# The second MLP of a pooled-attention and two-MLP kernel as seven block products, on tiles of 256 tokens

## The chip, the cores and the metric

The kernel runs on one core of a Trainium2 chip. The metric is the device time of one execution in microseconds; three runs of the kernel before gave 1746.33, 1746.94 and 1750.57 us, median 1746.94. The engines are TensorE (PE; its weight loads are shown apart as PEld), VectorE (DVE), ScalarE (ACT), GpSimd (POOL) and SyncE (SP, which only issues DMAs here).

## The reference

```python
def _attn_ref(q, k, v):                 # (8, 8, 576, 64): batch, heads, sequence, head
    k_p = k.reshape(B, H, Sp, 8, D).mean(axis=3)     # 72 pooled keys and values
    v_p = v.reshape(B, H, Sp, 8, D).mean(axis=3)
    scores = (1 / np.sqrt(D)) * np.matmul(q, k_p.transpose(0, 1, 3, 2))
    ...softmax...
    return np.matmul(attn, v_p)

def _moe_ref(x, w_in, w_out):           # x (4608, 512), w_in (512, 2048), w_out (2048, 512)
    h = x @ w_in
    g = np.where(h >= 1, h, np.where(h <= -1, 0, (h + 1) ** 2 / 4))
    return g @ w_out

def _moe2_ref(x, w_in, w_out):          # same shapes
    h = x @ w_in
    g = h * (1 / (1 + np.exp(-h)))
    return g @ w_out
```

The attention's output, 4608 tokens of 512 numbers, goes through the first MLP and then through the second. The moe weights come as 64-bit floats, which the kernel reads as pairs of 32-bit words.

## The kernel before

**Numbers.** Every big matrix is held as two f16 tiles, a high part and a low part, scaled by powers of two. A product of two such matrices is three matmuls into the same PSUM tile: high by high, high by low, low by high (`three`, lines 115 to 118). So all matmul counts below have a factor 3.

**Tiles and stages.** Tokens go in nine tiles of 512 (N). The attention prepares x for a tile of the first MLP. For each of 16 chunks m of 128 hidden numbers, `emit_h` makes 12 matmuls of 512 columns into a PSUM tile "h" (two buffers), ScalarE and VectorE make the activation g from it and split g into f16 halves, and three chunks later (LAG) `emit_yA` or `emit_yB` adds 12 more matmuls of 512 columns to the four output accumulators y0 to y3. So a tile is 384 matmuls. The main loop (line 1014) goes over the 16 x 18 steps of both MLPs without a break: the first nine tiles are the first MLP (`pre_A`, `min_A`, `mid_A`, `post_A`, `split_g`), the next nine the second (`act_B`, `split_g`). The first MLP's output goes to DRAM (`evac_yA`, ydram) and comes back a tile at a time (`tile_B`: one load "yin", four maxima, the scale by way of a pair of matmuls "all" on TensorE in `all_max`, and four splits). `big`, where y goes out and yin comes in, has one buffer.

**Weights of the second MLP.** They are prepared in steps during the first MLP (list `todo`, line 1009, spread over six tiles by the count in line 1047): load a piece of 1 MB (512 x 256 of w_in, 256 x 512 of w_out), five passes on ScalarE and VectorE that turn the 64-bit words into f32 (s0 to s4), then s5: scale and round on ScalarE, subtract on GpSimd, and write both halves to DRAM (d3, d4). For w_in each of eight pieces has its own scale, taken from a maximum that step s1 accumulates; for w_out one scale holds for all, and each piece is read twice, once to look at its maximum (`look`) and once to be converted. When the attention is done, its memory becomes free, and 8.4 MB of prepared weights are loaded into SBUF (lines 1041 to 1046).

**What sets the order.** The program is written in the order above; a scheduler of the framework then sets each engine's order, which an engine keeps: an instruction that waits holds up all that stand behind it. SP issues the DMAs in its own order.

Of the kernel before, what the change touches and what calls it, by code (L numbers as in the profile page):

```python
# [9 lines left out]
F32 = mybir.dt.float32  # L10
F16 = mybir.dt.float16
# [22 lines left out]
def tile_pooled_attention_two_mlps(  # L34
# [40 lines left out]
    w1p = ctx.enter_context(tc.tile_pool(name="w1", bufs=1))  # L75
# [76 lines left out]
    def w_scale(e, s, g):  # L152


        ts(g.bitcast(I32), g.bitcast(I32), 0x7FF00000, op0=ALU.bitwise_and)
        bits(s, g, -8.0, 2060)
        bits(e, g, 8.0, -1784)

    def steps(piece, dst, scale, loaded, mx=None, seen=None):
# [40 lines left out]
        def s5():  # L200
            x, s = t["x"], scale()
            hi, lo, *end = dst()
            nc.scalar.activation(out=x, in_=x, func=AF.Copy, scale=s)
# [72 lines left out]
    def weight_whole(w, e, dst, pieces):  # L276
# [16 lines left out]
        def scale():  # L293
# [30 lines left out]
    def split_steps(src, m4, e, s):  # L324
        hi, lo = new_x()

        def scale():
            m1 = sm.tile([128, 1], F32, tag="m1", name="m1")
            nc.vector.tensor_reduce(out=m1, in_=m4, axis=AX.X, op=ALU.max)
            to_scale(e, s, m1, FLOOR)  # L330

        return (hi, lo), [scale] + [lambda c=c: split(hi[:, c], lo[:, c], src[:, c], s) for c in range(KD)]
# [268 lines left out]
    w2 = [w1p.tile([128, 2, KF, 128], F16, name=f"wb{d}") for d in range(KD)]  # L601
# [7 lines left out]
    e1, e2, e3, e4 = col(len(cuts1)), col(KD), col(PIECES), col()  # L609
    e1m, e3m = col(), col()  # L610
# [36 lines left out]
    d3 = [dram.tile([128, KD, DFF], F16, name=f"d3{i}") for i in range(2)]  # L647
    d4 = [dram.tile([128, KF, DM], F16, name=f"d4{i}") for i in range(2)]

    def staged(views):  # L650
        shape = list(views[0].shape)
        t = [gp.tile([128, 2, N], F16, tag="g", name="hl").rearrange("p a n -> p (a n)") for _ in views]
        t = [x.rearrange("p (a b) -> p a b", a=shape[1]) for x in t]

        def end():
            for x, v_ in zip(t, views):
                nc.sync.dma_start(out=v_, in_=x)
        return t[0], t[1], end

    def dst3(p):  # L660
        hi, lo, end = staged([d[:, :, p * CW:(p + 1) * CW] for d in d3])
        if p < PIECES - 1:
            return hi, lo, end

        def both():
            end()
            largest(e3m, e3)
        return hi, lo, both

    def dst4(i):  # L670
        return staged([d[:, 2 * i:2 * i + 2] for d in d4])
# [23 lines left out]

    def load_y(t):
        y = big.tile([128, KD, N], F32, tag="big", name="yin")
        nc.sync.dma_start(out=y, in_=ydram[t])
        return y

    def tile_B(t):

        r = XT[NTILE + t] = small(e=1, s=1, c1=PIECES, ge=1, sg=1)
        held = {}

        def load():
            held["y"] = load_y(t)
            held["m4"] = sm.tile([128, KD], F32, tag="m4", name="m4b")

        def look(c):  # L710
            abs_max(held["m4"][:, c:c + 1], held["y"][:, c], AX.X)

        def more():
            r["x"], held["st"] = split_steps(held["y"], held["m4"], r["e"], r["s"])
            held["st"].pop(0)()
            ts(r["c1"], e3, r["e"], 2.0 ** -28, ALU.mult, ALU.mult)
            ts(r["ge"], e3m, r["e"], 2.0 ** -4, ALU.mult, ALU.mult)
            bits(r["sg"], r["ge"], -1.0, 254)

        return ([load] + [lambda c=c: look(c) for c in range(KD)] + [more]  # L720
                + [lambda: held["st"].pop(0)()] * KD)
# [82 lines left out]
    def act_B(s, r):  # L804
        ps = h_t.pop(s)
        p = s % KF // (KF // PIECES)
        g = g32_t[s] = up.tile([128, N], F32, tag="g", name="g32")
        nc.scalar.activation(out=g, in_=ps, func=AF.Silu, scale=r["c1"][:, p:p + 1])  # L808

    def split_g(s, r):  # L810
# [3 lines left out]
        if s < NTILE * KF:  # L814
            nc.scalar.copy(out=gh, in_=g)  # L815
            return nc.vector.tensor_tensor(out=gl, in0=g, in1=gh, op=ALU.subtract)  # L816
        else:
            nc.scalar.activation(out=gh, in_=g, func=AF.Copy, scale=r["sg"])  # L818
# [33 lines left out]
    def emit_yB(s, w):  # L852

        t, m = divmod(s, KF)
        if m == 0:
            new_acc(t)
# [243 lines left out]
```

## Time and profile before

| | us |
|---|---|
| median of three runs (1746.33 to 1750.57) | 1746.94 |
| the profiled execution, own time | 1752.34 |
| its span | 1750.4 |
| TensorE busy | 1620.5 (93%) |
| VectorE busy | 904.8 (52%) |
| ScalarE busy | 776.8 (44%) |
| GpSimd busy | 220.7 (13%) |

The first matmul of the second MLP starts at 990.1 us. Busy times are sums over instructions and average over quite different stages: attention and weight preparation run beside the first MLP until some 870 us, and GpSimd is idle after that. Matmuls are pipelined, so their durations (0.38 us for 512 columns) overlap; the time per matmul is the distance of their starts.

### The profile page before, as it was taken

Reading aid. Unit: us, or ns where it says so; the run is one execution under the profiler, and the core shown is the slowest. Engines: PE = TensorE matmul, PEld = TensorE weight load, DVE = VectorE, ACT = ScalarE, POOL = GpSimd, SP = SyncE. Lnnn points to the kernel's source line nnn. Section 1 sums busy time; section 2 is a strip of 40 time slices with the busy share of each in tenths; the row PEclk is TensorE's granted clock in tenths of the full one; section 3 lists DMA queues with packets and bytes.
Section 4 is the critical chain, followed back from the end, with each engine's and each line's share of the span. In section 5 each row is a group of like instructions: output and inputs, shape, how many; then the busy total and the mean of one; then the engine's idle time right before and its main releaser. Section 6 shows DMA issues by size and latency. Waiting matters only on the chain.

```text
span 1750.4 us, 21833 instructions
## 1 busy us (share of the span) xinstructions
PE 1620.5 (93%) x8594; PEld 757.5 (43%) x8594; DVE 904.8 (52%) x1714; ACT 776.8 (44%) x1215; POOL 220.7 (13%) x195
## 2 busy tenths in 40 slices
PE   4763789999998999999999999999999999999998
PEld 3321334444444444444444444444444444444443
DVE  8797778878788597886535331212121312122111
ACT  3575455665646556475434433333332323233232
POOL 5733412121221112112100000000000000000000
PEclk8786789999999999999999999999999999999999
DMA  9414655655659346342241010000000000000000
GB/s 283 127 57 119 138 130 128 149 127 125 154 125 269 89 131 148 90 120 61 55 187 49 10 63 25 25 25 24 25 25 25 25 24 25 25 25 25 0 25 24
DMA packets 206086, 144.55 MB, mean 83 GB/s; under 512 B 153120, under 2 KB 170528, under 8 KB 204832
## 3 DMA queue, kind: packets, MB, share of 16 engines
q1 hardware_dynamic: 205984, 143.16, 30.8%
q8 instruction: 67, 1.10, 0.3%
q14 instruction: 35, 0.29, 0.0%
HBM read 88.08 MB, written 27.26 MB: 66 GB/s over the span
## 4 chain that ended last, share of the span: by engine, by line
PE 64%; DVE 18%; ACT 7%; DMA 6%; issue 2%; POOL 1%; SPq 0%; ACTq 0%; POOLq 0%; DVEq 0%
PE hps L116 10%; PE hps L118 10%; PE hps L117 10%; PE y L863 7%; PE y L862 7%; PE y L861 7%; DVE sum L388 5%; PE y L116 3%; PE y L118 3%; PE y L117 3%; DVE g L816 2%; DVE g L762 2%; DMA raw<-in_moe_w_in_dram 1%; DVE xf L189 1%; DVE xf L195 1%
## 5 line engine op out<-in xcount | busy, mean ns | idle before, releaser
L819 DVE SCALAR_TENSOR_TENSOR g<-g,tsg,g 128x512 f16<-128x512 f32 x144 | 108.2, 751 | 479.6 <-ACT g L818 478.5
L808 ACT ACTIVATE g<-hps,tc 128x512 f32<-128x512 f32 x144 | 99.0, 687 | 504.7 <-PE hps L118 502.1
L116 PE MATMUL hps<-xh,wa 128*128 128x512 f16 x576 | 226.3, 393 | 40.0 <-DVE g L762 22.7
L117 PE MATMUL hps<-xl,wa 128*128 128x512 f16 x576 | 226.2, 393 | 0.0
L118 PE MATMUL hps<-xh,wa 128*128 128x512 f16 x576 | 224.3, 391 | 1.8 <-POOL wa L205 1.8
L116 PE MATMUL hps<-xh,wch 128*128 128x512 f16 x576 | 218.3, 379 | 0.0
L117 PE MATMUL hps<-xl,wch 128*128 128x512 f16 x576 | 218.3, 379 | 0.0
L118 PE MATMUL hps<-xh,wcl 128*128 128x512 f16 x576 | 218.3, 379 | 0.0
L861 PE MATMUL y<-wdh,g 128*128 128x512 f16 x576 | 218.3, 379 | 0.0
L862 PE MATMUL y<-wdl,g 128*128 128x512 f16 x576 | 218.3, 379 | 0.0
L863 PE MATMUL y<-wdh,g 128*128 128x512 f16 x576 | 218.3, 379 | 0.0
L117 PE MATMUL y<-g,wb 128*128 128x512 f16 x544 | 206.9, 380 | 2.3 <-DVE g L816 1.7
L118 PE MATMUL y<-g,wb 128*128 128x512 f16 x544 | 206.8, 380 | 0.0
L116 PE MATMUL y<-g,wb 128*128 128x512 f16 x544 | 203.5, 382 | 0.4 <-ACT y L849 0.4
L753 ACT ACTIVATE u<-u,trsg 128x512 f32<-128x512 f32 x128 | 91.9, 719 | 87.7 <-DVE u L89 87.7
L762 DVE SCALAR_TENSOR_TENSOR g<-hps,tc,u 128x512 f32<-128x512 f32 x136 | 101.5, 746 | 54.8 <-ACT u L753 53.8
L816 DVE TENSOR_TENSOR g<-g,g 128x512 f16<-128x512 f32 x128 | 97.2, 760 | 50.6 <-ACT g L815 49.1
L747 ACT ACTIVATE u<-hps,tch 128x512 f32<-128x512 f32 x128 | 87.0, 680 | 72.6 <-PE hps L118 72.3
L815 ACT CAST g<-g 128x512 f16<-128x512 f32 x128 | 78.5, 614 | 83.4 <-DVE g L762 81.0
L89 DVE TENSOR_SCALAR u<-u 128x512 f32<-128x512 f32 x144 | 75.8, 526 | 66.5 <-ACT u L747 66.1
L818 ACT ACTIVATE g<-g,tsg 128x512 f16<-128x512 f32 x144 | 103.8, 721 | 4.5
L117 PEld LDWEIGHTS <-wa 128*128 128x128 f16 x576 | 57.9, 101 | 96.1 <-issue 37.3
(171 smaller groups left out, 2047.2 us busy)
## 6 DMA issues: line engine op xcount, KB each, us to landing
raw<-in_moe_w_out_dram SPq DMA_DIRECT2D x24, 1024.0 KB
raw<-in_moe_w_in_dram SPq DMA_DIRECT2D x10, 1024.0 KB
raw<-in_k_dram SPq DMA_DIRECT2D x32, 288.0 KB
raw<-in_v_dram SPq DMA_DIRECT2D x32, 288.0 KB
y<-y SPq DMA_DIRECT2D x36, 256.0 KB
yin<-y SPq DMA_DIRECT2D x9, 1024.0 KB
out_dram<-osb SPq DMA_DIRECT2D x36, 256.0 KB
qt<-in_q_dram SPq DMA_DIRECT2D x32, 256.0 KB
```

Source lines behind the costliest of these rows:

```text
L116: nc.tensor.matmul(out=acc, lhsT=wh, rhs=xh, start=start, stop=False)
L117: nc.tensor.matmul(out=acc, lhsT=wh, rhs=xl, start=False, stop=False)
L118: nc.tensor.matmul(out=acc, lhsT=wl, rhs=xh, start=False, stop=stop)
L753: nc.scalar.activation(out=u_t[s], in_=u_t[s], func=AF.Square, scale=0.5 if s < KF else r["rsg"])
L762: return nc.vector.scalar_tensor_tensor(out=g, in0=h_t.pop(s), scalar=c_A(r, "c1", s), in1=u_t.pop(s), op0=ALU.mult, op1=ALU.max)
L808: nc.scalar.activation(out=g, in_=ps, func=AF.Silu, scale=r["c1"][:, p:p + 1])
L816: return nc.vector.tensor_tensor(out=gl, in0=g, in1=gh, op=ALU.subtract)
L818: nc.scalar.activation(out=gh, in_=g, func=AF.Copy, scale=r["sg"])
L819: nc.vector.scalar_tensor_tensor(out=gl, in0=g, scalar=r["sg"], in1=gh, op0=ALU.mult, op1=ALU.subtract)
L861: nc.tensor.matmul(out=a, lhsT=h_, rhs=w[0][:, m], start=st, stop=False)
L862: nc.tensor.matmul(out=a, lhsT=h_, rhs=w[1][:, m], start=False, stop=False)
L863: nc.tensor.matmul(out=a, lhsT=l_, rhs=w[0][:, m], start=False, stop=sp)
```

## The change

For a tile of 256 tokens the second MLP's two products are taken in blocks. x (512 x 256) and a piece of w_in (512 x 256) are cut into 2 x 2 blocks; sums and differences of the blocks are formed (`comb_a` for the weights, `comb_b` for x), seven block products are made instead of eight (`product`), and VectorE adds them up to the four blocks of h (c11, c12, c21, c22). The same is done for the output: sums of the blocks of g (z1 to z4, on GpSimd), seven products into y0 to y3 (`py`), and `evac_yB` adds them up.

The weights' combinations are made once, in the first MLP's time, and kept in DRAM: seven blocks of 256 columns a piece where there were four, as two halves. w_in now has one scale for all, with a look at each piece as w_out had. The first half of w_out's pieces (wd0 to wd3) and all of w_in's (wc0 to wc7) are loaded when the attention's memory is free, the other half (wd4 to wd7) when the first MLP's weights are released. The second MLP is a loop of its own: 18 tiles of 256 tokens, in two groups of four pieces each; the output products of a group are placed between the h products of the next.

```diff
-    w1p = ctx.enter_context(tc.tile_pool(name="w1", bufs=1))
+    wctx = ExitStack()
+    w2p = wctx.enter_context(tc.tile_pool(name="w2", bufs=1, side="right"))
+    w1p = wctx.enter_context(tc.tile_pool(name="w1", bufs=1, side="right"))
...
+            if fill:
+                fill(x)
+                return
...
+    def comb_a(z, a11, a12, a21, a22):
+        plus(z[1], a21, a22)
+        minus(z[2], z[1], a11)
+        minus(z[3], a11, a21)
+        minus(z[0], a12, z[2])
...
+    def staged(d, i, parts):
+        to = [[gp.tile([128, 2, N], F16, tag="g", name="hl").rearrange("p a n -> p (a n)") for _ in range(2)]
+              for _ in range(2)]
+        for a, b, x in parts:
...
+            nc.scalar.copy(out=hi, in_=x)
+            minus(lo, x, hi)
+        for j in range(2):
+            for k_, n in ((0, 4), (1, 3)):
+                nc.sync.dma_start(
...
+    def fill3(i, x):
+        b = x.rearrange("p (h c) (m f) -> p m h c f", h=2, m=2)
...
+        comb_a(z, b[:, 0, 0], b[:, 0, 1], b[:, 1, 0], b[:, 1, 1])
+        staged(d3, i, [(0, 2, b[:, 0]), (2, 3, z[0]), (3, 4, b[:, 1, 1]),
+                       (4, 7, z4[:, 1:4].rearrange("p n c f -> p (n c f)"))])
...
-    loads3, work3 = weight_in(moe2_w_in, e3, dst3, cuts3)
+    loads3, looks3, work3 = weight_whole(moe2_w_in, e3, fill3, [((0, KD), c) for c in cuts3])
...
+        def look():
+            m = sm.tile([128, 1], F32, tag="m1", name="m1")
+            abs_max(m, held["y"])
+            to_scale(r["e"], r["s"], m, FLOOR, 12)
...
+        return [load, look, sums_, lambda: part(0, 2, lambda: held["b"][:, :, 0]),
+                lambda: part(2, 3, lambda: held["b"][:, 1, 1]), lambda: part(3, 7, lambda: held["z"])]
...
+        def product(n, i):
+            p, tag = ((ps_h, "h"), (ps_a, "a"))[n // 2 % 2]
+            ps = p.tile([128, 4, 128], F32, tag=tag, name="hb")
+            for j in range(4):
+                w = w3[4 * q + j]
+                for k_ in range(2):
+                    three(ps[:, j], w[:, 0, i, k_], w[:, 1, i, k_], xh[:, i, k_], xl[:, i, k_],
+                          j == 0 and k_ == 0, j == 3 and k_ == 1)
+            return ps
...
+        def halves_of(i, x):
+            to = gt[i] = pool.tile([128, 2, N], F16, tag="g", name="g16")
+            split(to[:, 0], to[:, 1], x.rearrange("p j n -> p (j n)"), r["sg"])
...
+        nc.scalar.copy(out=u, in_=product(0, 0))
+        add(c11, u, product(1, 1))
+        act(c11)
+        halves_of(0, c11)
+        y(1)
+        add(u, u, product(2, 5))
+        y(1)
+        add(v, u, product(3, 6))
+        y(1)
+        p5 = product(4, 4)
+        add(c22, v, p5)
+        act(c22)
+        add(u, u, p5)
+        halves_of(3, c22)
...
+        plus(z1, c12, c22)
+        minus(z3, c11, c12)
+        minus(z2, z1, c11)
...
+            for j in range(4):
+                f, w = slice(128 * j, 128 * j + 128), w4[4 * q + j]
+                three_r(out, gh[:, f], gl[:, f], w[:, 0, i], w[:, 1, i], first and j == 0, last and j == 3)
...
+    todo = loads3 + looks3 + flat(work3) + loads4 + looks4 + flat(work4)
...
     wctx.close()
+    b2 = bctx.enter_context(tc.tile_pool(name="b2", bufs=1, side="right", reuse_waits="tile"))
+    for i in range(4, PIECES):
+        w4.append(b2.tile([128, 2, 7, 256], F16, name=f"wd{i}"))
+        nc.sync.dma_start(out=w4[i], in_=d4[:, i])
...
+    for t in range(NTB):
+        for q in range(2):
+            if t + 1 < NTB:
+                if q == 0:
+                    pend.extend(tile_B(t + 1))
+                for _ in range(3):
+                    pend.pop(0)()
+            ys = group_B(t, q, ys)
+            if q == 0 and t:
+                evac_yB(t - 1)
```

On SP, where the first MLP ends and the second begins, the order before is this (y7 and y8 are the first MLP's last outputs on their way to DRAM, yin_8974, yin_9554 and yin_10085 the x of tiles 0, 1 and 2 of the second MLP):

```order
L850 DMA y7_145<-y32_8938 128x512 x4
L698 DMA yin_8974<-y0_138 128x2048
L850 DMA y8_146<-y32_9522 128x512 x4
L698 DMA yin_9554<-y1_139 128x2048
L698 DMA yin_10085<-y2_140 128x2048
```

and in the changed kernel this (yin_9180 and yin_9712 are x of tiles 0 and 1, of 256 tokens each):

```order
L843 DMA y7_146<-y32_9144 128x512 x4
L859 DMA yin_9180<-y0_139 128x4x256
L843 DMA y8_147<-y32_9679 128x512 x3
L1178 DMA wd4_9693<-d4_138 128x3584
L843 DMA y8_147<-y32_9679 128x512
L1178 DMA wd5_9695<-d4_138 128x3584
L1178 DMA wd6_9697<-d4_138 128x3584
L1178 DMA wd7_9699<-d4_138 128x3584
L859 DMA yin_9712<-y0_139 128x4x256
```

Four loads of weights now stand between the last output of the first MLP and the x of tile 1.

On VectorE, at the same place, the second MLP's first instructions before are the low halves of g of tile 0 (line 819), and among them the maxima of tile 1's x (m4b_9556) and its scale (te_9549):

```order
L89 TENSOR_SCALAR y32_9522<-y3_8980,cy_9520 128x512
L819 SCALAR_TENSOR_TENSOR g16_9619<-g32_9586,tsg_8973,g16_9619 128x512
L107 TENSOR_REDUCE m4b_9556<-yin_9554 128x1 x4
L819 SCALAR_TENSOR_TENSOR g16_9650<-g32_9617,tsg_8973,g16_9650 128x512
L329 TENSOR_REDUCE m1_9717<-m4b_9556 128x1
L819 SCALAR_TENSOR_TENSOR g16_9681<-g32_9648,tsg_8973,g16_9681 128x512
L819 SCALAR_TENSOR_TENSOR g16_9712<-g32_9679,tsg_8973,g16_9712 128x512
L819 SCALAR_TENSOR_TENSOR g16_9755<-g32_9710,tsg_8973,g16_9755 128x512
L104 TENSOR_REDUCE te_9549<-all_9719 128x1
```

In the changed kernel (c_... are the sums of products, hb_... the products in PSUM, m1_9714 the maximum of tile 1's x, xl_9730 its low halves):

```order
L91 TENSOR_SCALAR y32_9679<-y3_9185,cy_9677 128x512
L904 TENSOR_TENSOR c_9731<-c_9732,hb_9765 128x512
L329 SCALAR_TENSOR_TENSOR g16_9792<-c_9731,tsg_9179,g16_9792 128x512
L109 TENSOR_REDUCE m1_9714<-yin_9712 128x1
L106 TENSOR_REDUCE te_9707<-all_9716 128x1
...
L329 SCALAR_TENSOR_TENSOR xl_9730<-yin_9712,ts_9708,xh_9729 128x512
L329 SCALAR_TENSOR_TENSOR xl_9730<-yin_9712,ts_9708,xh_9729 128x256
L904 TENSOR_TENSOR c_9732<-c_9732,hb_9795 128x512
L329 SCALAR_TENSOR_TENSOR xl_9730<-yin_9712,ts_9708,xh_9729 128x1024
L904 TENSOR_TENSOR c_9733<-c_9732,hb_9821 128x512
```

One addition stands ahead of tile 1's maximum, and the others of tile 0's first group (hb_9795 and on) behind it.

On TensorE, the pair "all" that spreads tile 1's maximum over the partitions stood before in the middle of tile 0, between an h chunk and an output block:

```order
L118 LDWEIGHTS wcl_8599
L118 MATMUL hps_9697<-xh_9155,wcl_8599 128x512
L103 MATMUL all_9719<-ident_87,m1_9717 128x128
L861 LDWEIGHTS g16_9681
L861 MATMUL y0_9557<-wdh_8600,g16_9681 128x512
```

In the changed kernel it stands behind four products and the first output block of tile 0 and ahead of the other three products of its first group:

```order
L969 LDWEIGHTS g16_9792
L969 MATMUL y0_9951<-wd3_8822,g16_9792 128x256
L105 MATMUL all_9716<-ident_90,m1_9714 128x128
L118 LDWEIGHTS wc0_8800
L118 MATMUL hb_9795<-xh_9269,wc0_8800 128x128
L119 LDWEIGHTS wc0_8800
L119 MATMUL hb_9795<-xl_9270,wc0_8800 128x128
```

So the step that once had most of a tile of other work ahead of it has five blocks now.

## Rows read from the trace of the kernel before

**Rows 1.** The page: busy time of the engines, and the clock granted to TensorE in 40 slices.

```profile
PE 1620.5 (93%) x8594; PEld 757.5 (43%) x8594; DVE 904.8 (52%) x1714; ACT 776.8 (44%) x1215; POOL 220.7 (13%) x195
...
PEclk8786789999999999999999999999999999999999
```

**Rows 2.** Stretches (us): length, busy time and instructions of each engine; granted clock, DMA share, GB/s.

```profile
240.00:850.00 610.00, 578.60 (x3632) 274.84 (x3631) 484.92 (x951) 351.54 (x589) 112.28 (x101) 0.99 0.53 130
876.00:896.00 20.00, 20.00 (x95) 9.07 (x93) 6.73 (x11) 7.49 (x12) 0.00 (x0) 1.00 0.99 374
900.00:1000.00 100.00, 100.00 (x466) 45.52 (x465) 42.31 (x75) 43.43 (x65) 0.00 (x0) 1.00 0.06 22
1100.00:1750.00 650.00, 645.67 (x2999) 293.89 (x2997) 146.04 (x253) 200.37 (x290) 0.00 (x0) 1.00 0.06 23
```

**Rows 3.** The chain of waits from 900 us: start, us, what.

```profile
951.15 0.22 PE all L103 x2
...
1615.95 0.22 PE all L103 x2
...
1746.63 0.75 DVE osb L89
```

**Rows 4.** Who waited, TensorE, 190 to 900 us: us in total, times, longest.

```profile
PE hps L116 <- DVE g L762: 22.7, 15, 3.8
```

**Rows 5.** Runs of small matmuls in order of time: start us, us, instruction, count.

```profile
524.90 0.42 PE L489 MATMUL att<-kT,qT 128*128 128x72 f16 x8
...
571.96 0.68 PE L489 MATMUL att<-kT,qT 128*128 128x72 f16 x16
...
799.40 0.95 PE L582 MATMUL att<-aT,v 72*64 72x64 f16 x48
```

**Rows 6.** Groups by line and form, TensorE weight loads: busy us, mean ns, idle before.

```profile
L861 PEld LDWEIGHTS <-g 128*128 128x128 f16 x576 | 56.4, 98 | 67.0
```

**Rows 7.** Groups by line and form on VectorE, ScalarE, GpSimd.

```profile
L819 DVE SCALAR_TENSOR_TENSOR g<-g,tsg,g 128x512 f16<-128x512 f32 x144 | 108.2, 751 | 479.6 <-ACT g L818 478.5
L762 DVE SCALAR_TENSOR_TENSOR g<-hps,tc,u 128x512 f32<-128x512 f32 x136 | 101.5, 746 | 54.8 <-ACT u L753 53.8
L816 DVE TENSOR_TENSOR g<-g,g 128x512 f16<-128x512 f32 x128 | 97.2, 760 | 50.6 <-ACT g L815 49.1 <-issue 1.1
...
L107 DVE TENSOR_REDUCE cols<-raw 128x1 f32<-128x1024 f32 x8 | 9.7, 1214 | 4.0 <-DMA raw<-in_moe_w_out_dram 4.0
L322 DVE SCALAR_TENSOR_TENSOR xl<-att,tsv,xh 128x256 f16<-128x256 f32 x8 | 3.8, 477 | 2.2 <-ACT xh L321 2.2
...
L818 ACT ACTIVATE g<-g,tsg 128x512 f16<-128x512 f32 x144 | 103.8, 721 | 4.5
...
L204 ACT CAST hl<-xf 128x1024 f16<-128x1024 f32 x16 | 16.6, 1040 | 0.1
...
L534 POOL TENSOR_TENSOR e<-e,e 128x288 f16<-128x288 f32 x64 | 50.9, 813 | 25.6 <-ACT e L533 25.2
L205 POOL TENSOR_TENSOR hl<-xf,hl 128x1024 f16<-128x1024 f32 x16 | 35.1, 2195 | 185.0 <-ACT hl L204 160.3 <-issue 24.6
```

**Rows 8.** In order of time, GpSimd and VectorE around 320 and 934 us.

```profile
319.91 2.13 POOL L205 TENSOR_TENSOR hl<-xf,hl 128x1024 f16<-128x1024 f32 x1 [21.14 <-issue]
...
320.39 1.93 DVE L89 TENSOR_SCALAR u<-u 128x512 f32<-128x512 f32 x1 [3.77 <-ACT u L747]
...
933.81 0.41 DVE L89 TENSOR_SCALAR u<-u 128x512 f32<-128x512 f32 x1
```

**Rows 9.** Line 816, VectorE: durations in ns, least/median/most.

```profile
L816 DVE TENSOR_TENSOR g<-g,g x128: 640/692/2204, 241.8 to 991.1; 128x512 f16<-128x512 f32 x128
```

**Rows 10.** In order of time, the DMA queue and VectorE around 926 us.

```profile
921.46 2.40 SPq L850 DMA_DIRECT2D y<-y  x4
926.11 0.32 SPq L698 DMA_DIRECT2D yin<-y  x1
...
931.43 2.47 DVE L107 TENSOR_REDUCE m4b<-yin 128x1 f32<-128x512 f32 x4 [2.02 <-DMA yin<-y]
```

More of the change, by code (lines that the diff above doesn't have):

```diff
@@ L201, in s5 @@
             x, s = t["x"], scale()
+            nc.scalar.activation(out=x, in_=x, func=AF.Copy, scale=s)
+            if fill:
+                fill(x)
+                return
             hi, lo, *end = dst()
-            nc.scalar.activation(out=x, in_=x, func=AF.Copy, scale=s)
             nc.scalar.copy(out=hi, in_=x)
@@ L274, in weight_out, with weight_whole @@
         ]
-    def weight_whole(w, e, dst, pieces):
+    def weight_whole(w, e, fill, pieces):
         wv = words(w)
@@ L322, in split @@
         return a, nc.vector.scalar_tensor_tensor(out=lo, in0=x, scalar=s, in1=hi, op0=ALU.mult, op1=ALU.subtract)
[L324 to L332, printed above, removed]
     att_ctx = ExitStack()
@@ L600, in tile_pooled_attention_two_mlps @@
     CW = DFF // PIECES
-    w2 = [w1p.tile([128, 2, KF, 128], F16, name=f"wb{d}") for d in range(KD)]
+    w2 = [w2p.tile([128, 2, KF, 128], F16, name=f"wb{d}") for d in range(KD)]
     cuts3 = [(p * CW, (p + 1) * CW) for p in range(PIECES)]
@@ L644, in tile_pooled_attention_two_mlps @@
     loads2, work2 = weight_out(moe_w_out, e2, dst2)
[L647 to L671, printed above, removed]
-    loads3, work3 = weight_in(moe2_w_in, e3, dst3, cuts3)
+    d3, d4 = (dram.tile([128, PIECES, 2, 7, 256], F16, name=n) for n in ("d3", "d4"))
+    def minus(out, a, b):
+        nc.gpsimd.tensor_tensor(out=out, in0=a, in1=b, op=ALU.subtract)
@@ L694, in consts_A @@
             ts(r["c1"], r["ch"], r["sg"], 2.0, ALU.mult, ALU.mult)
[L696 to L721, printed above, removed]
     acc_t = {}
@@ L802, in first_split @@
         slots.append(lambda: x)
[L804 to L808, printed above, removed]
     def split_g(s, r):
@@ L813, in split_g @@
         gh, gl = g_t[s] = to[:, 0], to[:, 1]
[L814 to L818, printed above, removed]
-            nc.vector.scalar_tensor_tensor(
-                out=gl, in0=g, scalar=r["sg"], in1=gh, op0=ALU.mult, op1=ALU.subtract
-            )
+        nc.scalar.copy(out=gh, in_=g)
+        return nc.vector.tensor_tensor(out=gl, in0=g, in1=gh, op=ALU.subtract)
     def yA(s, d, start, stop):
@@ L850, in evac_yA @@
             nc.sync.dma_start(out=ydram[t][:, d], in_=y[:, d])
[L852 to L856, printed above, removed]
-        gh, gl = g_t.pop(s)
-        for i in range(NI):
-            a, st, sp = acc_t[t][i], m == 0, m == KF - 1
-            h_, l_ = gh[:, i * 128:(i + 1) * 128], gl[:, i * 128:(i + 1) * 128]
-            nc.tensor.matmul(out=a, lhsT=h_, rhs=w[0][:, m], start=st, stop=False)
-            nc.tensor.matmul(out=a, lhsT=h_, rhs=w[1][:, m], start=False, stop=False)
-            nc.tensor.matmul(out=a, lhsT=l_, rhs=w[0][:, m], start=False, stop=sp)
+    TB = 256
```

210 lines of the change are left out of this document (150 added, 60 removed).

## The prediction

> **What bounds the kernel now.** The page first: TensorE is busy for 1620.5 of 1750.4 us (93%), VectorE for 52%, ScalarE for 44%, GpSimd for 13%, and the clock granted to TensorE is at its upper level (2.4 GHz) from some 260 us on [rows 1]. An average over stages says little here, so the stretches come next [rows 2]. From 900 us TensorE is busy in every microsecond (100.00 of 100.00), while VectorE works for 146 and ScalarE for 200 of the last 650 us and GpSimd for none. Whoever wants that half faster has to give TensorE less to do; VectorE, ScalarE and GpSimd have room. From 240 to 850 us it is another picture: TensorE 578.6 of 610 us, VectorE 484.9 (79%), ScalarE 351.5 (58%), GpSimd 112.3. TensorE idles 31.4 us there, and what ends most of its idle time is line 762 on VectorE, 15 waits, up to 3.8 us [rows 4]. So the first half is nearly TensorE's too, but VectorE is close behind. The chain of waits confirms the second half: nothing but matmuls, and the once-a-tile pair "all" gives its beat, 951.15 to 1615.95 us in eight tiles, 83.10 us a tile of 512 tokens [rows 3]. Nine tiles are 747.9 us.
>
> **TensorE in the second MLP.** Old: 16 x (12 + 12) = 384 matmuls of 512 columns and the pair "all" (0.22) a tile; (83.10 - 0.22) / 384 = 215.8 ns each. New, a tile of 256 tokens: 7 products x 8 pieces x 2 row blocks x 3 = 336 matmuls of 128 columns, and 7 x 8 x 3 = 168 of 256 columns, each with its own weight load. In columns this is 86,016 for the old 98,304: seven eighths. What a short matmul takes is the question. No full-array f16 matmul of 128 or 256 columns stands in the trace; the nearest are the attention's of 72 columns with full 128x128 loads: 8 of them 0.42 us, 16 of them 0.68 us [rows 5], so 0.26 / 8 = 32.5 ns for each further load and matmul. Straight through 72 (32.5 ns) and 512 (215.8 ns) it is 0.417 ns a column: 55.8 ns for 128, 109.2 ns for 256. A tile is 336 x 55.8 + 168 x 109.2 + 0.22 = 37.3 us, eighteen are 671.8 us: **76.1 us less**. Ends: the load of a weight block is shown as 98 ns [rows 6]. If loads did not overlap at all with each other, each 128-column matmul would take 98 ns and the gain would turn into 336 x 18 x 42.2 ns - 76.1 us = 179 us of loss. The run of 72-column pairs contradicts that, since each of its loads is also about 0.1 us long and they follow at 32.5 ns; I take 55.8. It rests on runs of 16, and 48 of half width in 0.95 us; the new kernel's are 24.
>
> The Trainium skill ("TensorE: Matmul & The Clock Gate", Back-to-back issue gap) speaks against the change: in a stream of load and matmul pairs both count, some 81 ns at 128 columns and some 131 ns at 512. By it a tile would take 336 x 25.2 ns = 8.5 us longer and the kernel 152 us, and be slower than before. The trace disagrees with the second figure (215.8 ns) and, with 32.5 ns at 72 columns, hardly allows the first.
>
> **The engines beside it.** Per 256 tokens VectorE gets 14 additions out of PSUM (0.746), 14 halves (0.751), 7 of 256 columns at the end (0.477), one maximum (1.21), the halves of x (0.746 + 0.477 + 1.28 by 1.05 ns a column) and some ten tiny ones, 1.5 [rows 7]: 29.5 us of 37.3. ScalarE: 24 of 0.72 and 2.8 for x and the end, 20 us. GpSimd, by the line through 0.813 us for 288 and 2.195 us for 1024 columns (0.27 us and 1.88 ns a column): 8 x 1.23 + 4 x 0.75 = 12.9 us. GpSimd was idle in this half; now it shares something with VectorE. At 319.91 us a GpSimd subtraction of 2.13 us starts; a VectorE instruction that takes 0.41 us otherwise (at 933.81) starts at 320.39 and takes 1.93, ending 0.28 us after it [rows 8]. Line 816, two operands in SBUF, has 692 ns as median and 2204 as most [rows 9], while line 762, one operand in PSUM, stays at 746 [rows 7]. So VectorE's 17 halves a tile are exposed and its additions are not. If they fall on a running GpSimd operation by chance (12.9 / 37.3 = 35%) and wait half of one (0.6 us), that is 3.6 us: VectorE at 33 of 37.3. Ends: 29.5 (no loss) and 29.5 + 12.9 = 42.4 (all in turn, TensorE 5.1 us late a tile). A product's PSUM bank is wanted again four products later, some 8 us after its end, so waits of 1 us are swallowed; the order of VectorE's instructions keeps the additions near their products. I take **5 us** in all.
>
> **The first MLP.** All of the weights' preparation runs there. A piece used to cost GpSimd one subtraction of 1024 columns (2.2 us); now four of 256 and subtractions of 512, 256, 256 and 768: 3.0 + 4.4 = 7.4. Sixteen pieces: +84 us on the 112.3. ScalarE: 1792 columns for 1024 in four copies, at 1040 ns a thousand [rows 7] with their starts about 1.2 us more, 19 us in all (58% to 61%). VectorE: eight more looks of 1.21 = 9.7 us; the running maximum inside s1 and seven of eight scales go, so 0 to 9.7. DMA: 8 MB more to load, 32 more writes, at a share of 0.53 now [rows 2]. Bounds for TensorE: from -31 us (its idle time gone) to +84 (each GpSimd microsecond on its path). Line 816 lost 128 x 68 ns = 8.7 us beside 112 us of GpSimd; with the other forms that read SBUF twice (lines 89, 91, 189, 195, 322) I reckon two and a half times that, 0.2 us per microsecond: 17 us of VectorE, which ends TensorE's waits most often but not always. I take **13 us**.
>
> **The seam.** Before, tile 1's x is wanted 83 us into the second MLP. Now it is wanted after two groups (7 products of 1.34 us, then 7 and 7 output blocks of 1.31), 28 us in, and its "all" stands on TensorE right behind four products and one output block of tile 0: 4 x 1.34 + 1.31 = 6.7 us after the seam, some 8 with the wait for the first activation. Its load yin stands on SP behind the last y writes and the four loads wd4 to wd7, which wait for the first MLP's weights to be released. These are 3.67 MB and with y's 1 MB take 4.7 / 0.374 = 12.5 us at the 374 GB/s of a dense stretch [rows 2]. Writes and reload of y alone took from 921.46 to 931.43 us with the queue to themselves [rows 10]. So yin lands some 18 us after the seam, the maximum takes 1.2: TensorE stands about 11 us at "all". On VectorE the maximum is ahead of the additions of four finished products; behind it the halves of x wait for GpSimd's four sums (3.0), so PSUM frees late, 4 us more. **15 us**; ends 2 (the load overtakes) and 22. The tail behind the last matmul, 0.75 us on VectorE and a write [rows 3], stays about as long: nothing.
>
> **Sum.** Own time of the profiled run 1752.34 us (span 1750.4 and 1.94 around it), 5.4 above the median 1746.94 of the runs. 1752.34 - 76.1 + 5 + 13 + 15 = 1709.2; on the median's scale **1704 us**, 2.5% faster.
>
> **Rivals.**
> - Seam and first MLP cost next to nothing (5 us in all): 1752.34 - 76.1 + 5 - 5.4 = 1676. For it: both are off TensorE's path by busy time. Against: in-order queues, and waits of up to 3.8 us already [rows 4]. 15%.
> - The first MLP pays more, 50 us, because a ScalarE copy of a sum stands in front of the next tile's activation and waits for GpSimd: 1741. For it: 84 us of new work in a chain of ScalarE, GpSimd, ScalarE; against: GpSimd is at 18% and goes to 32%. 12%.
> - Slower: VectorE and GpSimd take turns in the second MLP, and VectorE's 42.4 us replace TensorE's 37.3. 5.1 x 18 = 92 us for my 5: 1791. From 39.9 us a tile on the change loses. For it: rows 8 and 9; against: only 13 of VectorE's 29.5 us are exposed. 10%.
> - Slower: loads don't hide, 98 ns a short matmul: 1704 + 255 = 1959. 4%, the 72-column runs against it.
>
> That the work is not cut at all is excluded by the instructions: 504 matmuls a tile.
>
> **How the numbers follow.** The forecast has 55% (own range 1685 to 1730); 4% are left for what I don't see. The range 1678 to 1755 leaves out the two slow rivals and the best corner. Less than 0.3% (5.2 us) can't be told from no change. Faster: most of the forecast (53), the first rival (15), half of the second (6), odds (5): 0.79. Same 0.06. Slower: 10 and 4 and a little: 0.15.
>
> **What would show it.** A beat of 37.3 us between "all" matmuls (39 or more: port or loads); matmul starts 55.8 ns apart inside a product; TensorE's idle time in 240 to 850 us at 44 us rather than 31; an idle stretch of about 11 us before the "all" of tile 1, ended by VectorE's maximum behind DMA; VectorE's halves with a mean of 0.95 rather than 0.75 us. I am wrong if the beat is above 39.9, or the first MLP loses over 50 us.

## The result, and the profile after

The changed kernel takes **1703.8 us** (median of 4 runs, 1701.4 to 1704.6), the kernel before 1747.3 in the same session: ratio 0.9746, 95% interval 0.9729 to 0.9763. The forecast was 1704. A total that fits can still be made of terms that don't, so the terms come first. The profiled execution of the changed kernel has 1703.5 us and so lies at its median; that of the kernel before lay 5.4 us above the median of its runs.

The page of the changed kernel, busy time of the engines and TensorE's granted clock, which answers to [rows 1]:

```profile
PE 1549.1 (91%) x14214; PEld 1054.7 (62%) x14214; DVE 1241.3 (73%) x2218; ACT 886.8 (52%) x1425; POOL 569.8 (33%) x523
...
PEclk8786789999999999999999989999999999999999
```

TensorE has 71 us less to do in 5600 more instructions; VectorE gained 336 us of work and GpSimd 349. From the seventh slice on only one is below nine tenths of the upper clock, the 24th (978 to 1021 us), which holds the seam, the place where the first MLP ends and the second begins. The stretches, in the columns of [rows 2]:

```profile
240.00:850.00 610.00, 579.03 (x3627) 274.30 (x3625) 495.65 (x924) 368.40 (x638) 200.80 (x213) 0.99 0.58 154
1005.00:1010.00 5.00, 0.00 (x0) 0.00 (x0) 0.00 (x0) 0.00 (x0) 0.00 (x0) 0.64 0.97 387
1010.00:1015.00 5.00, 2.07 (x16) 2.01 (x17) 2.32 (x9) 0.34 (x1) 2.82 (x4) 0.50 0.08 29
1015.00:1020.00 5.00, 5.00 (x79) 5.00 (x77) 4.73 (x9) 2.10 (x4) 0.00 (x0) 0.84 0.04 10
1080.00:1580.00 500.00, 492.18 (x6651) 465.50 (x6649) 366.30 (x625) 243.22 (x372) 188.27 (x157) 1.00 0.09 29
```

First, the first MLP: GpSimd has 88.5 us more in 240 to 850 us (84 was reckoned), and TensorE is busy for 579.0 us where it was 578.6. Its idle time is 31 us as before, not the 44 forecast. Second, from 1005 to 1010 us every engine stands still while the DMA engines run at 387 GB/s, and in the next 5 us the granted clock is at its lower level (0.50). Third, in the steady part TensorE idles 7.8 of 500 us.

TensorE's matmuls in order of time (start us, us, engine, line, operation; in brackets, where there is one, the idle time before it and what ended it): the first three of the second MLP's first product, then the first matmul of a product in a later tile, of the output block behind it and of the next product. Below them a group of weight loads (busy us, mean ns, idle us before), and one view by operation of the pair "all" (least/median/most ns, first and last start), which comes once a tile of 256 tokens:

```profile
995.06 0.22 PE L118 MATMUL hb<-xh,wc 128*128 128x128 f16 x1
995.12 0.22 PE L119 MATMUL hb<-xl,wc 128*128 128x128 f16 x1
995.17 0.22 PE L120 MATMUL hb<-xh,wc 128*128 128x128 f16 x1
...
1300.12 0.22 PE L118 MATMUL hb<-xh,wc 128*128 128x128 f16 x1
...
1301.46 0.27 PE L967 MATMUL y<-wd,g 128*128 128x256 f16 x1
...
1302.77 0.22 PE L118 MATMUL hb<-xh,wc 128*128 128x128 f16 x1
```

```profile
L119 PEld LDWEIGHTS <-wc 128*128 128x128 f16 x2016 | 197.8, 98 | 2.5
```

```profile
L105 PE MATMUL all<-ident,m x30: 275/275/275, 1078.7 to 1612.7; 128*128 128x128 f32 x30
```

A product of 24 matmuls takes 1301.46 - 1300.12 = 1.34 us, 55.8 ns each, and an output block of 12 takes 1.31 us, 109.2 ns each; the weight loads of 98 ns are hidden behind them. The beat, from the "all" of tile 3 to that of tile 17, is (1612.7 - 1078.7) / 14 = 38.1 us, not 37.3. What takes most of the 0.8 us is one wait a tile, in the list of TensorE's waits (us in total, times, longest):

```profile
PE y L967 <- DVE ob L980: 10.4, 16, 1.5
```

The second of a tile's output products goes into the PSUM bank y1, which VectorE still reads in the fifth and sixth of its seven closing additions (line 980) for the tile before. On VectorE these stand among low halves of g, which need the high halves that ScalarE makes, and ScalarE in turn waits for GpSimd's sums (the second line below). Groups by line, in the columns of [rows 6]:

```profile
L329 DVE SCALAR_TENSOR_TENSOR g<-c,tsg,g 128x512 f16<-128x512 f32 x252 | 226.4, 901 | 86.9 <-ACT g L328 86.9
...
L328 ACT ACTIVATE g<-c,tsg 128x512 f16<-128x512 f32 x252 | 177.6, 718 | 83.7 <-POOL c L654 51.5
L904 DVE TENSOR_TENSOR c<-c,hb 128x512 f32<-128x512 f32 x252 | 167.8, 680 | 71.2 <-PE hb L120 70.8
...
L651 POOL TENSOR_TENSOR c<-c 128x512 f32<-128x512 f32 x108 | 163.7, 1530 | 2.8
```

VectorE's halves have a mean of 901 ns where they had 751 [rows 7]; the additions out of PSUM have 680, less than the 746 that the prediction took for them from line 762. The seam on the queue, VectorE and TensorE, in order of time:

```profile
995.84 0.44 SPq L1178 DMA_DIRECT2D wd<-d  x1
996.33 0.53 SPq L843 DMA_DIRECT2D y<-y  x1
996.90 1.92 SPq L1178 DMA_DIRECT2D wd<-d  x3
1004.16 0.55 SPq L859 DMA_DIRECT2D yin<-y  x1
```

```profile
1011.66 1.22 DVE L109 TENSOR_REDUCE m<-yin 128x1 f32<-128x1024 f32 x1 [10.66 <-DMA yin<-y]
```

```profile
1012.93 0.79 PE L105 MATMUL all<-ident,m 128*128 128x128 f32 x2 [10.61 <-DVE m L109]
```

yin is issued behind four loads of 0.9 MB and has landed when the maximum starts at 1011.66 us; TensorE stands for 10.6 us at the "all" of tile 1. From the first product (995.1) to the "all" of tile 3 (1078.7) it takes 83.6 us. By the order of the program 672 matmuls of 128 columns, 252 of 256 and two pairs "all" lie between them, 672 x 0.0558 + 252 x 0.1092 + 0.44 = 65.5 us: the seam cost 18, of which 10.6 is this wait. Of the rest, 3.8 us are other waits of TensorE, for line 980 and for halves. Some 2 us are the clock, an estimate from the granted clocks above: 0.50 up to 1015 us and 0.84 in the 5 us after are half the upper clock for some 3.6 us of work (2 up to 1015 us and 1.6 behind it), which costs about half of that.

### The profile page after: what moved, and what is told of

Same layout as the page of the kernel before. It is cut to its first block, busy times and chain, and to the rows that moved or that the text cites. A ratio compares the mean times of both kernels' runs of the same rounds, so it can differ in the third digit from the quotient of the medians.

```text
span 1701.7 us, 34324 instructions
## 1 busy us (share of the span) xinstructions
PE 1549.1 (91%) x14214; PEld 1054.7 (62%) x14214; DVE 1241.3 (73%) x2218; ACT 886.8 (52%) x1425; POOL 569.8 (33%) x523
## 4 chain that ended last, share of the span: by engine, by line
PE 32%; DVE 26%; issue 15%; ACT 11%; POOL 9%; DMA 7%; SPq 0%; DVEq 0%; POOLq 0%; ACTq 0%
DVE sum L386 5%; PE hps L118 4%; PE hps L120 4%; PE hps L119 4%; PE y L118 4%; POOL c L651 4%; PE y L120 4%; DMA yin<-y 4%; PE y L119 4%; DVE g L329 4%; POOL c L654 2%; DVE xl L329 2%; ACT g L328 2%; ACT c L907 2%; DVE c L904 2%
## 5 line engine op out<-in xcount | busy, mean ns | idle before, releaser
L119 PE MATMUL hb<-xl,wc 128*128 128x128 f16 x2016 | 349.8, 219 | 0.0
L118 PE MATMUL hb<-xh,wc 128*128 128x128 f16 x2016 | 349.8, 219 | 0.0
L120 PE MATMUL hb<-xh,wc 128*128 128x128 f16 x2016 | 349.8, 219 | 0.0
L329 DVE SCALAR_TENSOR_TENSOR g<-c,tsg,g 128x512 f16<-128x512 f32 x252 | 226.4, 901 | 86.9 <-ACT g L328 86.9
L967 PE MATMUL y<-wd,g 128*128 128x256 f16 x1008 | 274.7, 273 | 11.9 <-DVE ob L980 10.4
L969 PE MATMUL y<-wd,g 128*128 128x256 f16 x1008 | 274.8, 273 | 1.0 <-DVE g L329 0.9
L968 PE MATMUL y<-wd,g 128*128 128x256 f16 x1008 | 274.7, 273 | 0.0
L907 ACT ACTIVATE c<-c,tc 128x512 f32<-128x512 f32 x144 | 103.0, 717 | 256.3 <-DVE c L904 256.3
L328 ACT ACTIVATE g<-c,tsg 128x512 f16<-128x512 f32 x252 | 177.6, 718 | 83.7 <-POOL c L654 51.5
L904 DVE TENSOR_TENSOR c<-c,hb 128x512 f32<-128x512 f32 x252 | 167.8, 680 | 71.2 <-PE hb L120 70.8
L119 PEld LDWEIGHTS <-wc 128*128 128x128 f16 x2016 | 197.8, 98 | 2.5
L118 PEld LDWEIGHTS <-wc 128*128 128x128 f16 x2016 | 197.8, 98 | 2.1
L120 PEld LDWEIGHTS <-wc 128*128 128x128 f16 x2016 | 197.8, 98 | 0.2
L651 POOL TENSOR_TENSOR c<-c 128x512 f32<-128x512 f32 x108 | 163.7, 1530 | 2.8
L651 POOL TENSOR_TENSOR yin<-yin 128x256 f32<-128x256 f32 x72 | 52.6, 752 | 289.0 <-DMA yin<-y 287.7
```

The costliest lines, as they stand in the source:

```text
L118: nc.tensor.matmul(out=acc, lhsT=wh, rhs=xh, start=start, stop=False)
L119: nc.tensor.matmul(out=acc, lhsT=wh, rhs=xl, start=False, stop=False)
L120: nc.tensor.matmul(out=acc, lhsT=wl, rhs=xh, start=False, stop=stop)
L328: a = nc.scalar.activation(out=hi, in_=x, func=AF.Copy, scale=s)
L329: return a, nc.vector.scalar_tensor_tensor(out=lo, in0=x, scalar=s, in1=hi, op0=ALU.mult, op1=ALU.subtract)
L651: nc.gpsimd.tensor_tensor(out=out, in0=a, in1=b, op=ALU.subtract)
```

## The experiments

### The load of tile 1 ahead of the last weights

```diff
+    pend.extend(tile_B(1))
+    pend.pop(0)()
     ...
-        nc.sync.dma_start(out=w4[i], in_=d4[:, i])
+        with tc.issue_after(XB[1]["load"].ins):
+            nc.sync.dma_start(out=w4[i], in_=d4[:, i])
     ...
-                if q == 0:
+                if q == 0 and t:
     ...
-                for _ in range(3):
+                for _ in range(2 if t + q == 0 else 3):
```

> Edit: the load of tile 1's x (yin) is issued on SP ahead of the four weight loads wd4 to wd7 instead of behind them; the first MLP's order is untouched. Theory (the seam is the DMA queue: yin waits behind 3.67 MB): TensorE's idle time ahead of tile 1's pair 'all' falls from 10.6 us to about 2, yin lands some 8 us after the first product instead of 16.6, the granted clock does not fall there, and the kernel gains 9 to 12 us on 1703.8: about 1693. Rival (VectorE and GpSimd hold the seam, with one maximum, four sums and the halves of x in front of five additions): the idle time only moves behind 'all', gain under 3 us, 1701 or more.

**1690.6 us**, 13.2 less than the changed kernel, a little more than the 9 to 12 expected; against before 0.968 (0.9652 to 0.9708). The queue, VectorE and TensorE at the seam, in order of time:

```profile
999.56 0.55 SPq L859 DMA_DIRECT2D yin<-y  x1
1000.16 2.85 SPq L1181 DMA_DIRECT2D wd<-d  x4
```

```profile
1003.50 1.22 DVE L109 TENSOR_REDUCE m<-yin 128x1 f32<-128x1024 f32 x1 [2.19 <-DMA yin<-y]
```

```profile
1004.78 0.49 PE L105 MATMUL all<-ident,m 128*128 128x128 f32 x2 [2.14 <-DVE m L109]
```

The wait shrinks from 10.6 to 2.1 us, and from the first product to the "all" of tile 3 it is 72.6 us for 83.6, so 7 of the seam's 18 us remain. The loads wd then come later without anybody waiting longer for them. The bytes are the same in both kernels, so the order on the queue makes the difference. It acts twice: yin needs the buffer `big`, and SP waits 2.7 us instead of 5.2 until the last y has left it; and the maximum of yin starts 3.9 us after the issue instead of 7.5. What a second buffer would give was not tried.

### The second output bank later

```diff
-    ORDER = [0, 3, 4, 6, 5, 1, 2]
+    ORDER = [0, 6, 3, 4, 5, 1, 2]
```

> Edit: ORDER of the output products 0, 6, 3, 4, 5, 1, 2 instead of 0, 3, 4, 6, 5, 1, 2, so that the accumulator y1, which the closing additions of the tile before free last but one, is wanted 2.65 us later, and y3, freed earlier, takes its place. Theory (the one wait a tile, 0.5 to 1.5 us for line 980, is y1 being still read): the beat of 'all' falls from 37.97 to 37.3 us, the gain is 17 x 0.65 = 11 us: about 1693. Rival (VectorE is simply late, whatever is wanted first): the wait comes back at y3 or y1 with 0.5 us or more, gain under 3 us.

**1690.5 us**, 13.3 less (0.9681, 0.9658 to 0.9704). VectorE's order is the same; only TensorE comes to the bank y1 later, and takes y3, which is free earlier, in its place. The pair "all", by operation:

```profile
L105 PE MATMUL all<-ident,m x30: 275/275/275, 1078.1 to 1600.7; 128*128 128x128 f32 x30
```

The beat is 522.6 / 14 = 37.3 us, the term of the forecast to the tenth, and no wait for line 980 is left in the list. The halves still take 901 ns: they were slow without being the loss.

### Both

> Edit: both of the above, the load of tile 1's x first and the other order of output products. Theory: the two losses stand at different places, so the gains add up: 20 to 23 us, about 1682, beat 37.3 and no idle stretch over 3 us at the seam. Rival (what TensorE saves in one place it waits for in the other, because VectorE is the pace-maker): under 14 us together, above 1690.

Both edits at once: **1679.4 us** (1676.5 to 1681.5), 0.9614 of the kernel before (0.959 to 0.9639): 24.4 less than the changed kernel, and the gains nearly add up (13.2 + 13.3 = 26.5). The stretch from 1080 to 1580 us:

```profile
1080.00:1580.00 500.00, 500.00 (x6785) 474.56 (x6783) 373.09 (x632) 246.01 (x375) 192.83 (x160) 1.00 0.09 30
```

TensorE is busy in all of the 500 us.

### Without GpSimd's sums of the activations

The four sums a group are left out, and the halves made of blocks in their place.

```diff
-        plus(z1, c12, c22)
-        minus(z3, c11, c12)
-        minus(z2, z1, c11)
...
-        halves_of(4, z1)
-        halves_of(6, z3)
+        halves_of(4, c12)
+        halves_of(6, c11)
...
-        halves_of(5, z2)
-        minus(z4, c21, z2)
+        halves_of(5, c22)
...
-        halves_of(2, z4)
+        halves_of(2, c21)
```

> Edit: GpSimd's four sums z1 to z4 of each group are left out; the halves are made from c12, c11, c22 and c21 in their place, so that VectorE and ScalarE have the same instructions. Output order as in the changed kernel. Theory (the port that GpSimd and VectorE share delays VectorE's halves, mean 901 ns for 751, and by that the closing additions): halves back to 750 to 770 ns, the wait for line 980 gone, beat 37.3, about 11 us faster. Rival (the closing additions are late by VectorE's order of instructions alone): halves faster all the same, but the wait stays at 0.4 us or more and the beat at 37.8 or more.

**1689.0 us** in one run, 14.9 less. Groups by line and form, 1080 to 1580 us, and the pair "all":

```profile
L329 DVE SCALAR_TENSOR_TENSOR g<-c,tsg,g 128x512 f16<-128x512 f32 x187 | 132.9, 746 | 26.0 <-ACT g L328 26.0
L904 DVE TENSOR_TENSOR c<-c,hb 128x512 f32<-128x512 f32 x188 | 126.4, 684 | 113.2 <-PE hb L120 113.1
```

```profile
L105 PE MATMUL all<-ident,m x30: 275/275/275, 1075.5 to 1598.2; 128*128 128x128 f32 x30
```

With GpSimd down from 188 to 40 us in the stretch, the same halves take 746 ns and the beat is 37.3 us. So the additional 155 ns of each half come from GpSimd's sums beside them. The Trainium skill (SBUF — State Buffer, section "SBUF: two separate sides") says that VectorE operations with two SBUF inputs and GpSimd operations that read SBUF take an exclusive pair of ports in turn. The traces agree with it: 901 against 746 ns for the halves, which read SBUF twice, and 680 against 684 for the additions, which read PSUM. But this experiment takes away two things, the sharing and the wait for the sums themselves. The kernel with the output bank moved, which leaves both and gains nearly as much, says that neither harms TensorE here unless a bank hangs on it.

### An eighth product, read by nobody

```diff
+        product(7, 0)
         c21 = v
```

> The changed kernel, plus an eighth h product in every group (24 matmuls of 128 columns, read by nobody), so that TensorE gets back the h products' saving and VectorE, ScalarE and GpSimd keep all the work of the seven-product scheme. In the changed kernel 24 such matmuls take 1.34 us; there are 36 groups. Theory (TensorE is the pace-maker of the second MLP, and the matmuls left out are what the change saves): 36 x 1.34 = 48 us more, less some 8 to 12 us if the extra 1.34 us covers the wait of 0.5 to 1 us that each tile has for the closing additions: 1738 to 1753 us, a beat of 'all' of 40.0 to 40.7 us for 38.0. Rival (VectorE with GpSimd paces the tiles, and TensorE has time to spare): the product runs in waits that are there now, under 24 us more, below 1728 us, with a beat below 39.3 us.

**1742.2 us** in one run, 38.4 more. The pair "all":

```profile
L105 PE MATMUL all<-ident,m x30: 275/275/275, 1083.2 to 1646.0; 128*128 128x128 f32 x30
```

A beat of 562.8 / 14 = 40.2 us, 2.1 more than in the changed kernel and 2.9 more than without the wait (2 x 1.34 = 2.7 us is the product's own time in a tile's two groups). The granted clock is 1.00 from 1080 to 1580 us in both. So TensorE sets the pace: a product put back costs its own time, and 0.2 us a tile is all that is left of waits. The matmuls left out are the gain.

### The first MLP without the sums of the weights

```diff
-        comb_a(z, b[:, 0, 0], b[:, 0, 1], b[:, 1, 0], b[:, 1, 1])
-        staged(d3, i, [(0, 2, b[:, 0]), (2, 3, z[0]), (3, 4, b[:, 1, 1]),
-                       (4, 7, z4[:, 1:4].rearrange("p n c f -> p (n c f)"))])
+        staged(d3, i, [(0, 2, b[:, 0]), (2, 3, b[:, 1, 0]), (3, 4, b[:, 1, 1]), (4, 7, x2[:, 256:1024])])
```

(and the same for w_out.)

> The changed kernel without the sums of the weights: GpSimd's additions in the preparation are left out, and the halves that were made from sums are made from plain blocks of the same weights (the same tiles, the same work on ScalarE, VectorE and the queues), so the second MLP multiplies other numbers and its output is not the reference's. GpSimd has some 88 us less in the first MLP. Theory (GpSimd's sums there are hidden altogether, and the first MLP did not pay for them): 1700 to 1707 us, and the first product of the second MLP starts within 2 us of the 995.1 us that it has in the changed kernel. Rival (the sums cost the 13 us that I reckoned, 0.2 us or less for each us of GpSimd, and something else in the change gave back as much): the first product starts 6 to 17 us earlier, 1687 to 1698 us.

**1708.4 us** (1705.6 to 1711.4), 4.5 more than with the sums. GpSimd had 48 us less in 240 to 850 us (152.8 for 200.8), not the 88 that the expectation says: the halves' subtractions stay. The rival has fallen, since nothing comes earlier; the theory's range was missed as well, by 1.4 us in the total and by 2.6 us in the first product's start. By operation, the first start is the seam:

```profile
L118 PE MATMUL hb<-xh,wc x2016: 219/219/314, 999.7 to 1688.7; 128*128 128x128 f16 x184
```

The 4.6 us are all in the first MLP (999.7 for 995.1). The changed kernel and the five above have the same instructions there, and their first product comes at 992.6 to 996.4 us, so this is a little more than scatter. What makes it is not shown; less work on GpSimd came out no earlier.

### The sums of the weights made four times

```diff
-        comb_a(z, b[:, 0, 0], b[:, 0, 1], b[:, 1, 0], b[:, 1, 1])
+        for _ in range(4):
+            comb_a(z, b[:, 0, 0], b[:, 0, 1], b[:, 1, 0], b[:, 1, 1])
```

(and the same for comb_b.)

> The changed kernel with each sum of the weights made four times over in the preparation (the same result): GpSimd gets three times the additions' work more, some 200 us or more, in the first MLP. Theory (hidden; GpSimd had 161 us of work more to give in the 610 us between 240 and 850, and the additions do not slow VectorE's operations much): TensorE's busy time between 240 and 850 us falls by less than 5 us, the total is 1703 to 1712 us, and VectorE's busy time there rises by less than 30 us. Rival (each us of GpSimd in the first MLP costs 0.15 us, as my +13 for 84 us had it): 25 to 40 us more, 1729 to 1744 us. If GpSimd itself is full, it ends above that.

**1742.6 us**, 38.8 more. The total lies in the rival's range, but at another price: GpSimd got some 155 us more and not 200, so a microsecond of it cost 0.25 and not 0.15. GpSimd is not full over the stretch (335.6 of 610 us), though it works for 61.5 of the 90 us from 780 to 870. The stretch, waits on TensorE and on ScalarE:

```profile
240.00:850.00 610.00, 555.64 (x3417) 261.11 (x3416) 490.86 (x888) 348.32 (x607) 335.60 (x382) 0.96 0.53 149
```

```profile
PE hps L118 <- DVE g L769: 31.8, 10, 8.0
PE y L118 <- ACT g L815: 8.0, 6, 3.5
...
PE y L119 <- DVE g L816: 7.0, 5, 3.4
```

```profile
ACT hl L681 <- POOL z L651: 15.4, 7, 4.2
```

In the changed kernel itself the same wait of ScalarE, and the first of TensorE's, are

```profile
ACT hl L681 <- POOL z L651: 0.8, 1, 0.8
```

```profile
PE hps L118 <- DVE g L767: 15.9, 6, 4.4
```

VectorE's instruction with two SBUF inputs in the first MLP (line 816, 814 in the changed kernel), 240 to 980 us, in the kernel before, the changed kernel and this experiment:

```profile
L816 DVE TENSOR_TENSOR g<-g,g 128x512 f16<-128x512 f32 x125 | 95.1, 761 | 48.6 <-ACT g L815 47.0 <-issue 1.1
```

```profile
L814 DVE TENSOR_TENSOR g<-g,g 128x512 f16<-128x512 f32 x126 | 96.0, 762 | 47.6 <-ACT g L813 43.9 <-issue 1.8 <-POOL z L651 0.9
```

```profile
L816 DVE TENSOR_TENSOR g<-g,g 128x512 f16<-128x512 f32 x117 | 94.3, 815 | 34.4 <-ACT g L815 32.6 <-POOL z L651 1.5
```

The price does not start at once: the changed kernel and the last experiment show none, and this one does. A piece's sums take 4 x 0.75 = 3.0 us, and in the changed kernel they are done when ScalarE comes to copy them (0.8 us of waiting in all). Made four times, 12 us, they often are not: ScalarE stands at the copy for 15.4 us, the activations queued behind it are late, and TensorE's waits for activations grow. VectorE's instructions beside GpSimd are longer too (815 for 762 ns); how much of TensorE's waiting comes by either way is not shown, nor where between 3 and 12 us the price begins. Of the 38 us, 23 are TensorE's busy time lost in 240 to 850 us, in which the mean granted clock fell from 0.99 to 0.96 as well; how the loss divides between the waits and the clock isn't settled.

### One scale for the first weights, in the kernel before

```diff
-    loads3, work3 = weight_in(moe2_w_in, e3, dst3, cuts3)
+    loads3, looks3, work3 = weight_whole(moe2_w_in, e3, dst3, [((0, KD), c) for c in cuts3])
...
-    todo = loads3 + flat(work3) + loads4 + looks4 + flat(work4)
+    todo = loads3 + looks3 + flat(work3) + loads4 + looks4 + flat(work4)
```

> The kernel before, with one part of the change alone: the second MLP's first weights are looked at whole and get one scale for all pieces, where before has a scale for each of eight pieces; products and tiles are those of before. It asks what gave back the time that I had put on the first MLP. Theory A (the single scale shortens the way from the last pieces of the weights to the second MLP): 2 to 10 us faster than before, 1737 to 1745 us, with the first product of the second MLP before 990 us (990.1 us in before). Theory B (nothing in it counts; the looks are hidden as the sums are): within 2 us of 1747.4. Theory C (the looks cost VectorE's time): slower by 4 us or more.

**1756.8 us**, 1.0049 (1.0031 to 1.0067): theory C, 9 us slower. The single scale, with its looks and its second loading, does cost; which of these costs is not separated. Since the changed kernel has it too and its first MLP is only some 3 us longer (worked out below), something else in the change must give most of it back.

### The halves in two instructions, with the single scale and alone

```diff
-            nc.scalar.copy(out=hi, in_=x)
-            nc.gpsimd.tensor_tensor(out=lo, in0=x, in1=hi, op=ALU.subtract)
+            n = x.shape[1] // (2 if hi.shape[1] * hi.shape[2] == 1024 and end else 1)
+            for a in range(0, x.shape[1], n):
+                h_, l_, x_ = hi[:, a:a + n], lo[:, a:a + n], x[:, a:a + n]
+                nc.scalar.copy(out=h_, in_=x_)
+                nc.gpsimd.tensor_tensor(out=l_, in0=x_, in1=h_, op=ALU.subtract)
```

> The kernel before with the single scale of the run before last (1756.8 us), and with the halves of the second MLP's weights made by two instructions of 512 elements on ScalarE and two on GpSimd, where it has one of 1024 each; products and tiles are those of before. The changed kernel has such shorter instructions too. Theory (in-order engines: GpSimd's 2.1 us subtraction holds up the attention's operations that TensorE waits for, and the shorter ones gave back what the single scale cost): 1746 to 1751 us, first products of the second MLP 6 us or more earlier than with the single scale alone (993.7 us). Rival (the length of these instructions counts for nothing): 1754 to 1760 us.

**1749.3 us**, 1.0005 of the kernel before (0.9994 to 1.0017) and 7.5 less than with the single scale alone. By operation, the second MLP's products (the first start is the seam) and GpSimd's subtraction, then the products with the single scale alone:

```profile
L116 PE MATMUL hps<-xh,wch x576: 379/379/379, 984.8 to 1729.3; 128*128 128x512 f16 x192
```

```profile
L208 POOL TENSOR_TENSOR hl<-xf,hl x32: 1150/1162/1607, 318.8 to 809.8; 128x512 f16<-128x512 f32 x32
```

```profile
L116 PE MATMUL hps<-xh,wch x576: 379/379/379, 993.7 to 1738.2; 128*128 128x512 f16 x192
```

> The kernel before with the two instructions for one alone (eight scales as before). Theory as for the run beside it: 1738 to 1742 us, 6 us or more faster than before (1747.5). Rival: within 3 us of before.

**1746.2 us**, 0.9989 (0.9978 to 0.9999), 2.7 less: here the rival holds. Instructions of 1.16 us for 2.13 give back most of what the single scale costs, and little where there is no single scale. That the shorter instructions do it is shown by the medians; by which queue is not: the waits on TensorE differ by up to 3 us in several places, and no one of them carries 7.5 us. Of the 8.9 us between the two starts above, part is scatter between two executions: in the first 240 us, before the first of the split instructions (318.8 us), TensorE was already busy for 147.3 us instead of 145.2. And no run tries the split in the changed kernel itself, whose subtractions have 256 to 768 columns.

## Why the prediction was right, and where it was not

On the scale of the medians the seam of the kernel before lies at 1745.5 (end of its last matmuls, 4.9 us before the span's end) - 747.9 - 5.4 = 992.2 us; the changed kernel's first product comes at 995.1. This puts the 5.4 us by which the profiled execution is above its median ahead of the seam: in the four kernels with the old second MLP it takes 762.2 to 763.1 us from its first product to the end, so the scatter lies in the first half.

- **TensorE, -76.1 us: right.** 37.3 us a tile in the three kernels without the wait, 55.8 ns per load and matmul. The straight line through the attention's runs of 16 [rows 5] held for streams of thousands. The rule of the Trainium skill ("TensorE: Matmul & The Clock Gate", Back-to-back issue gap), some 81 ns at 128 columns, is refuted here by 55.8. The rival that counted 98 ns for each load is refuted by the same 55.8 ns.
- **The engines beside it, +5: too small.** The beat gives 534.0 - 522.6 = 11.4 us over the fourteen tiles behind the seam, and the experiment that removes the wait 13.3 in all. The premise on speed was good: halves at 0.95 us were forecast, 0.90 came, and the additions are not slowed (680 ns beside GpSimd's sums, 684 without). GpSimd's sums were taken too cheap, at 12.9 us a tile where they took 14.6, without harm to TensorE. The failed sentence is that waits of 1 us are swallowed because a product's bank is wanted again four products later. That holds for the products' banks. The output's bank y1 is wanted again at once, in the second output product, and I did not look at it.
- **The first MLP, +13: too large, the mis-sized term.** Measured 995.1 - 992.2 = 3 us, within the scatter of some 4 us that the same instructions show. I took 0.2 us of VectorE per microsecond of GpSimd from the long cases of line 816 [rows 9], 17 us in all, and let most of it end in waits on TensorE. That step failed: with 88.5 us more of GpSimd the instruction's mean went from 761 to 762 ns, and VectorE's busy time in 240 to 850 us rose by 10.7 us, of which the eight looks are 9.7; ScalarE waited 0.8 us in all for a sum. A price near the one that I took appears only with a further 155 us of GpSimd (38.8 us, 0.25 each). In the kernel before, the experiments name two parts that count: the single scale (+9) and the shorter instructions (-7.5 beside it); that they also make up the 3 us here is not shown.
- **The seam, +15: near.** It cost 18. The mechanism, place and wait (11 us forecast, 10.6 measured) were right, and the experiment shows the order on the queue as its cause. What I had not foreseen is the clock, which is at its lower level behind the wait: the pair "all" takes 0.79 us there, 0.39 in a later tile.
- **Sum.** -76.1 + 11.4 + 3 + 18 = -43.7, measured -43.5. The errors, +6, -10 and +3, nearly cancel; that the total met the forecast to a microsecond is luck. That it is faster, and by an amount of this size, is not luck: the largest term was right.

Of the rivals, the first MLP's (a copy of a sum in front of the next activation) shows only beyond this change's dose. VectorE and GpSimd taking turns slows VectorE but leaves TensorE the bound: VectorE is busy for 366 of 500 us.

## What to carry to other kernels

Where TensorE bounds a stage and its neighbours have room, fewer columns in more and shorter matmuls can pay in full, as they did here, as long as the time from start to start stays a straight line in columns; check that on any run of small matmuls that the trace has. Then look for the few places where a stage's end is not covered: a bank that is wanted again at once, and a load queued behind larger ones whose data is not wanted yet. Both took a few lines here and gave 24 us more, over half of what the whole scheme gave. The 88.5 us of work put on GpSimd cost little while each piece was finished before an in-order engine asked for it, and a further 155 us cost a quarter of that time, so ask for the latency of one piece, not only for the busy share.

## What the runs showed of the hardware that was not expected

- TensorE did nothing for 10.6 us, up to 1012.9. The granted clock was 0.64 from 1005 to 1010 us, 0.50 (its lower level, 1.2 GHz) in the next 5 us and 0.84 in the 5 after. After a wait of 2.1 us at the same place it stayed at 1.00 (1000 to 1010 us) in the version with the load first, and was 0.82 and 0.83 in the version with both edits.
- A weight load of 98 ns before each matmul of 128 columns stays hidden at 55.8 ns from start to start, over 6048 of them.
- GpSimd's additions beside them make VectorE's operations with two SBUF operands 20% longer on average (901 for 746 ns), at a GpSimd share of 38%, and leave those that read PSUM alone (680 for 684).
